# Summing attention weights and both halves of the values' product inside PSUM

## The chip, the cores and the metric

The kernel runs on one core of a Trainium2 chip. The metric is device time in microseconds (us) of one execution. Engine names in the profile: PE is the matrix engine TensorE (PEld its weight loads), DVE is VectorE, ACT is ScalarE, POOL is GpSimd, SP issues the DMAs.

## The reference, cut to what matters

Four batches of 576 tokens, eight heads of 64 features. Rotary attention comes first, then a mixer on its result: a low-rank mix over the sequence, then two dense layers with a ReLU. Only the end of the attention is touched here:

```python
scores = scores - np.max(scores, axis=-1, keepdims=True)
attn = np.exp(scores)
attn = attn / (np.sum(attn, axis=-1, keepdims=True) + 1e-09)
return np.matmul(attn, v).astype(np.float32)
```

Inputs and outputs are float32, and the mixer's weights are float64.

## The kernel before, in words

**Tiling.** A batch has four pairs of heads (index hp). A pair has five tiles of queries: four of 128 (t = 0 to 3), for each of which both heads have a softmax tile of their own, and a last one (t = NT = 4) in which the last 64 queries of both heads share one tile of 128. So a pair has nine softmax tiles, and a batch 36. For each, PE makes the scores, DVE the maximum (nmx), ACT the exponential (p), with the row sum as a second output of the same instruction (`accum_out=sm`).

**Batch 0 is plain.** With PLAIN = HV = 4 all four pairs of batch 0 take the plain path: p is transposed by PE, and the values' product runs in float32, one PE instruction for each chunk of 128 keys (5 chunks, the last of 64 keys). In the trace each float32 product stands as two passes. The values lie in v32, a float32 view of the tile va.

**Batches 1 to 3 carry halves.** ACT rounds p to float16 (the high half), POOL subtracts (the low half), and one transposing DMA turns both into nine chunks pt. The values are also split into a high and a low half of float16 (tile va, high and low side by side). The product sums high weights times (high | low) values over chunks 0 to 4, and low weights times high values over the remaining chunks. Since the 576 keys don't fill five chunks, the fifth holds 64 keys of the high weights and 64 of the low ones; the tile vb, and the upper 64 rows of va's last chunk, hold the values shifted to suit. `twice` in load_v makes them by three DMAs.

**values, lines 841 to 918.** The output tile pv is one PSUM bank: two heads, two halves, 64 columns. For each head the chunks 0 to 4 write 128 columns (two halves of 64), the other four 64. `evac` follows: rs (sum plus 1e-9, times the values' scale) and rc (its reciprocal), which need only sm; then xs, a DVE reduction that adds the two halves out of PSUM into SBUF; then xt, xs times rc, as one DVE instruction or two ACT ones, whichever the plan expects to end first. `turn` transposes xt on PE and splits it for the mix.

**load_v, lines 689 to 746.** For each of the batches 1 to 3 two raw tiles are loaded, each all 576 rows of 256 columns: a DMA of 512 KB in runs of 1 KB and one of 64 KB. ACT sums their squares, PE and DVE make the scale of that, ACT and DVE or POOL write the halves, and `twice` copies.

**What sets the order.** Up to the end of batch 3 everything is recorded by the class Plan, which knows for each instruction what memory it touches, and is then placed by a list scheduler with its own estimates of durations (`cost`), waits (`lag`) and of the DMA queue (`place`). Six passes backward and forward choose the order; each engine then runs its instructions strictly in that order. A PSUM bank is one unit of dependence: the next tile's product can't begin before the last reader of pv is done. The groups of PE instructions of one head stay together (`group`). While batch b's attention runs, the mixer of batch b - 1 fills PE; after the last batch's attention only the mixer is left.

Line 304 is `Plan.emit`, which all planned instructions share, so the rows of the profile are told apart by their tiles.

Of the kernel before, what the change touches and what calls it, by code (L numbers as in the profile page):

```python
# [21 lines left out]
#: Attention weights are carried times this, so that their low halves stay normal in float16.  # L22
PSC = 2.0**14
# [4 lines left out]
XM = 1  # L28
# [8 lines left out]
class Plan:  # L37
    """Records the program in its natural order, then emits it in the order in which a model of
    the core would start it: what comes first goes first, what comes later fills the gaps.
    Instructions depend on each other by the memory that they touch."""  # L40
# [28 lines left out]
    @contextmanager  # L69
    def later(self, level):  # L70
        """What others go before."""
        was, self.level = self.level, level
        yield
        self.level = was

    @contextmanager
    def sooner(self, steps):
        """What goes before the given number of instructions in front of it."""
        was, self.ahead = self.ahead, steps
        yield  # L80
        self.ahead = was

    def region(self, ap):
# [40 lines left out]
    def cost(calls):  # L124
        """How long they hold the engine."""
# [33 lines left out]
    def shares(calls):  # L159
        """Whether they hold the SBUF port that VectorE and GpSimd share."""  # L160
# [8 lines left out]
    def gap(self, dev, t, d):  # L169
        """The first time from t on at which dev is free for d."""  # L170
# [21 lines left out]
    def place(self, ways, before):  # L192
        """The way that is done first: when it starts, the calls, what they hold."""
        found = []
        for calls in ways:
# [5 lines left out]
            if eng == "sync":  # L201
# [7 lines left out]
                # Transfers go in the order of issue: an early issue would be in others' way.  # L209
# [25 lines left out]
    def lag(a, b):  # L235
        """From the end of an instruction to the start of one that waits for it."""
# [23 lines left out]
    def forward(self, order):  # L260
        """As early as they can be, in the given order."""
# [11 lines left out]
    def backward(self):  # L273
        """How late they could start, the last ones first."""
# [53 lines left out]
def tile_rope_attention_then_mixer(ctx, tc, qk, v, tab, u_in, v_in, w1, w2, out):  # L328
# [17 lines left out]
    def tmp(tag, shape, bufs, name):  # L346
        """A small tile for a while."""
# [29 lines left out]
    # Hidden units by chunks; before there are any, the first batch's attention has the room.  # L377
# [10 lines left out]
    # Queries of the even and the odd head, their high and low parts, the former before a pad of  # L388
    # zeros, the latter after one; keys' high parts, twice, and their low parts over zeros.
# [34 lines left out]
    def copy(o, i, engines):  # L424
        """A rounding copy."""
# [26 lines left out]
    def scaled_low(o, i, sc, hi, engines):  # L452
        """What the high half leaves of the scaled values; may overwrite these."""
# [21 lines left out]
    # Scales that are of use after the first batch's attention.  # L475
# [11 lines left out]
        # The exponent halved is the root's.  # L487
# [90 lines left out]
    def pieces(t):  # L578
        """Memory for halves of groups as they come in."""
# [6 lines left out]
    # A slot may not serve once float32 values are there.  # L586
# [7 lines left out]
    def weight(g):  # L594
        """A group from float64 to float32, and its sums of squares."""
# [55 lines left out]
    def weight_scale(w):  # L651
        """The scale of w1, or of the columns 128 (w - 1) .. of w2."""
# [36 lines left out]
    def load_v(b):  # L689
        """v in float16 halves, its rows twice over: chunk j holds the keys 128 j .. modulo S."""  # L690
        raws = []
        cuts = ((P, slice(0, NT)), (REM, slice(NT, NC)))
        first = 0
        if b == 0:
            first = HV * P
            for e in range(2):
                cc = slice(e * HV * 64, (e + 1) * HV * 64)
                r = v32[:, :, e, 0:HV * 64]
# [4 lines left out]
        hw = min(DM // 2, DM - first)  # L703
        for o in range(first, DM, max(hw, 1)):
            cc = slice(o, o + hw)
            r = next(raw_ring)[:, 0:NC * hw].rearrange("p (c d) -> p c d", d=hw)
            nc.sync.dma_start(r[:, 0:NT, :], v[b, 0:MAIN, cc].rearrange("(c p) d -> p c d", p=P))
            nc.sync.dma_start(r[0:REM, NT, :], v[b, MAIN:S, cc])
            nc.gpsimd.memset(r[REM:P, NT, :], 0.0)
            raws.append((r, cc))  # L710
        if not raws:
            return
        am = tmp("amv", [2], 2, f"amv{b}")

        def squares():
            junk = vb.rearrange("p j d -> p (j d)")[:, 0:NC * hw]
            for i, (r, cc) in enumerate(raws):
                nc.scalar.activation(
                    out=junk.rearrange("p (c d) -> p c d", d=hw), in_=r, func=AF.Square,
                    accum_out=am[:, i:i + 1],  # L720
                )
            am1 = am[:, 0:1]
            if len(raws) > 1:
                am1 = tmp("amv1", [1], 2, f"amv1{b}")
                nc.vector.tensor_reduce(out=am1, in_=am, axis=AX.X, op=ALU.add)
# [3 lines left out]
        def split(i):  # L729
            r, cc = raws[i]  # L730
            sc = state[b]["vsc"]
            for n, c in cuts:
                scaled(va[:n, c, 0, cc], r[:n, c, :], sc[:n], "AD")
            for n, c in cuts:
                scaled_low(va[:n, c, 1, cc], r[:n, c, :], sc[:n], va[:n, c, 0, cc], "DP")
# [6 lines left out]
        cols = slice(first, DM)  # L742
        squares()
        for i in range(len(raws)):
# [3 lines left out]
    def load_qk(b, hp):  # L748
        """Queries and keys of two heads."""
# [7 lines left out]
    def rope(b, hp, x):  # L757
        """Their rotation; the first batch's products are in plain float32."""
# [9 lines left out]
    def halves(b, hp, x):  # L768
        """Halves of 12 bits: contraction rows [high; low] of the queries against [high; high] and
        [low; 0] of the keys."""  # L770
        r = state[b, hp]["raw"][x]
        for e in range(2):
# [6 lines left out]
            if QS and b == 0 and x == 0:  # L779
                # The scores' scale, so that their maxima serve as they are.  # L780
# [60 lines left out]
    def values(b, hp, t, pts, sm):  # L841
        """The heads' values for one tile of queries: t, or NT for both heads' last REM."""
        plain = plain_pv(b, hp)
        nj = NC if plain else NJ
        cols = slice(hp * P, (hp + 1) * P)
        for e, pt in enumerate(pts):
            d = cols if t == NT else slice(hp * P + e * 64, hp * P + e * 64 + 64)
            o = pv.rearrange("p e k d -> p k e d") if t == NT else pv[:, e]
            with nc.group():
                for j in range(nj):  # L850
                    k = P if not plain or j < NT else REM
# [458 lines left out]
```

## Time and profile before

| | us |
|---|---|
| runs before (3), median | 709.77 |
| lowest and highest of them | 707.08, 715.2 |
| span of the profiled execution | 707.0 |
| PE busy | 661.2 (94%) |
| DVE busy | 517.0 (73%) |
| ACT busy | 399.7 (57%) |
| POOL busy | 214.1 (30%) |

The page gives no whole time for the profiled execution beside its span of 707.0; the run of 707.08 lies nearest to it, so some 0.1 us lie around the span. Busy PE is modelled: instructions overlap, so what one costs is read from the starts of its neighbours and not from its duration.

### The profile page before, as it was taken

Reading aid. Unit: us, or ns where it says so; the run is one execution under the profiler, and the core shown is the slowest. Engines: PE = TensorE matmul, PEld = TensorE weight load, DVE = VectorE, ACT = ScalarE, POOL = GpSimd, SP = SyncE. Lnnn points to the kernel's source line nnn. Section 1 sums busy time; section 2 is a strip of 40 time slices with the busy share of each in tenths; the row PEclk is TensorE's granted clock in tenths of the full one; section 3 lists DMA queues with packets and bytes.
Section 4 is the critical chain, followed back from the end, with each engine's and each line's share of the span. In section 5 each row is a group of like instructions: output and inputs, shape, how many; then the busy total and the mean of one; then the engine's idle time right before and its main releaser. Section 6 shows DMA issues by size and latency. Waiting matters only on the chain.

```text
span 707.0 us, 14026 instructions
## 1 busy us (share of the span) xinstructions
PE 661.2 (94%) x5312; PEld 538.6 (76%) x5312; DVE 517.0 (73%) x1120; ACT 399.7 (57%) x959; POOL 214.1 (30%) x201
## 2 busy tenths in 40 slices
PE   2999899997998898999999999999999999999998
PEld 1888788775776676888778878777878778777776
DVE  6888888887899998886778896777799873530220
ACT  3777677766775865645746666437766673230210
POOL 0320201012334345625434646124553452000000
PEclk9999999999899999999999999999999999999999
DMA  8767263248365558735777576427855664000000
GB/s 257 240 227 222 75 211 96 96 134 193 83 123 110 144 86 166 147 98 134 119 173 159 117 154 124 129 79 144 182 118 118 114 100 79 18 1 26 10 10 25
DMA packets 160468, 85.57 MB, mean 121 GB/s; under 512 B 131024, under 2 KB 149456, under 8 KB 160400
## 3 DMA queue, kind: packets, MB, share of 16 engines
q1 hardware_dynamic: 160400, 84.68, 50.6%
q8 instruction: 41, 0.67, 0.4%
q14 instruction: 27, 0.22, 0.1%
HBM read 41.70 MB, written 4.72 MB: 66 GB/s over the span
## 4 chain that ended last, share of the span: by engine, by line
PE 60%; DVE 20%; DMA 8%; ACT 6%; issue 4%; POOL 1%; SPq 0%; ACTq 0%; POOLq 0%; DVEq 0%
PE mm L304 40%; PE s L304 10%; PE pv L304 9%; DMA pt<-p 5%; DVE wt L304 5%; DVE raw L304 3%; ACT p L304 3%; DVE nmx L304 3%; DMA raw<-qk 1%; DVE st L304 1%; DMA x<-w 1%; DVE rs L304 1%; DVE xt L304 1%; DVE kl L304 1%; ACT room L304 1%
## 5 line engine op out<-in xcount | busy, mean ns | idle before, releaser
L304 PEld LDWEIGHTS <-wt 128*128 128x128 f16 x2688 | 253.5, 98 | 67.9 <-issue 3.0
L304 PE MATMUL mm<-room,wt 128*128 128x288 f16 (+1 forms) x1472 | 218.8, 298 | 0.1
L304 POOL TENSOR_TENSOR p<-p,p 128x576 f16<-128x576 f32 x108 | 149.1, 1385 | 195.7 <-ACT p L304 156.8
L304 PE MATMUL mm<-u,wt 128*128 128x288 f16 x1344 | 184.1, 286 | 1.9 <-DVE room L304 1.8
L304 DVE TENSOR_REDUCE nmx<-s 128x1 f32<-128x576 f32 x144 | 108.0, 752 | 28.6 <-PE s L304 25.6
L304 PE MATMUL s<-kh,st 128*128 128x288 f32 x320 | 106.8, 352 | 20.9 <-DVE st L304 14.0
L304 ACT ACTIVATE room<-mm 128x288 f16<-128x288 f32 (+3 forms) x156 | 63.0, 410 | 108.5 <-PE mm L304 107.7
L304 ACT ACTIVATE p<-s,nb 128x576 f32<-128x576 f32 x108 | 79.5, 737 | 36.7 <-DVE nb L304 33.4
L304 PE MATMUL s<-kl,st 128*128 128x288 f32 x320 | 95.4, 316 | 0.8 <-DVE kl L304 0.8
L304 DVE SCALAR_TENSOR_TENSOR room<-mm,room 128x288 f16<-128x288 f32 x112 | 50.7, 453 | 54.2 <-ACT room L304 53.4
L304 PE MATMUL pv<-va,pt 128*128 128x128 f16 (+5 forms) x760 | 83.3, 244 | 6.5 <-DMA pt<-p 6.0
L304 PEld LDWEIGHTS s<-kh,st 128*128 128x128 f32 x320 | 62.3, 197 | 32.6 <-DVE st L304 15.1
L304 ACT ACTIVATE p<-p 128x576 f16<-128x576 f32 x108 | 72.9, 681 | 11.4 <-DMA pt<-p 9.7
L304 PEld LDWEIGHTS <-pt 128*128 128x128 f16 x972 | 55.1, 98 | 18.1 <-DMA pt<-p 9.8
L304 PEld LDWEIGHTS s<-kl,st 128*128 128x128 f32 x320 | 63.0, 199 | 2.5 <-DVE kl L304 1.1
L304 DVE TENSOR_TENSOR raw<-raw,cs 128x1152 f32<-128x1152 f32 (+1 forms) x29 | 39.5, 1365 | 6.9 <-DMA raw<-qk 6.9
L304 DVE TENSOR_REDUCE xs<-pv 128x128 f32<-128x256 f32 x60 | 25.1, 419 | 24.7 <-PE pv L304 24.1
L304 DVE SCALAR_TENSOR_TENSOR ob<-mm,so,x 128x288 f32<-128x288 f32 x28 | 14.3, 510 | 37.1 <-PE mm L304 37.1
L304 PE MATMUL mm<-x,wt 128*128 128x288 f32 x128 | 35.7, 422 | 0.6 <-DVE x L304 0.6
L304 PE MATMUL pv<-vb,pt 128*128 128x64 f16 (+1 forms) x432 | 31.5, 196 | 1.7 <-DMA vb<-va 1.7
L304 PE MATMUL mm<-ident,p 128*128 128x128 f32 (+1 forms) x180 | 32.2, 294 | 0.9 <-ACT pt L304 0.5
L304 ACT ACTIVATE p<-s,nmx 128x576 f32<-128x576 f32 x36 | 26.5, 736 | 11.5 <-DVE nmx L304 11.2
(122 smaller groups left out, 816.0 us busy)
## 6 DMA issues: line engine op xcount, KB each, us to landing
raw<-qk SPq DMA_DIRECT2D x30, 576.0 KB, 4.7
wt<-w SPq DMA_DIRECT2D x23, 512.0 KB, 5.4
x<-w SPq DMA_DIRECT2D x9, 512.0 KB, 3.5
out_t<-ob SPq DMA_DIRECT2D x32, 144.0 KB, 1.8
kh<-kh SPq DMA_DIRECT2D x30, 144.0 KB, 2.6
raw<-vt SPq DMA_DIRECT2D x6, 512.0 KB, 4.9
pt<-p SPq DMA_TRANSPOSE x108, 3.3
vb<-va SPq DMA_DIRECT2D x6, 256.0 KB, 3.5
```

What stands on the lines that cost most here:

```text
L304: getattr(getattr(nc, eng), op)(*a, **k)
```

## The change

pv becomes two heads of 66 columns (64 sums, the sum of weights, a pad). va is split into two tiles: vh, whose heads are 66 columns wide with ones behind the 64 values, and vl with the low halves; vb gets the width of vh. In batches 1 to 3 each of the chunks 0 to 4 now takes two PE instructions that add into the same columns, one of 65 columns (high values and the ones) and one of 64 (low values); the other four take 65 columns. So a head's group has 14 instructions where it had nine. The exponential has no second output there, xs is gone, rs reads the sums from pv, and xt reads pv. The last tile of a plain pair takes two float32 products of 64 columns for each chunk where it took one of 128. load_v loads raw tiles of 256 rows and all columns (the last 64 rows in two parts of columns), and `twice` has four DMAs.

```diff
-    pv = psum.tile([P, 2, 2, 64], F32, name="pv")
+    pv = psum.tile([P, 2, 66], F32, name="pv")
...
-    va = cst.tile([P, NC, 2, DM], F16, name="va")
-    vb = cst.tile([P, NJ - NC, DM], F16, name="vb")
-    v32 = va.bitcast(F32)
+    vh = cst.tile([P, NC, NH, HW], F16, name="vh")
+    vl = cst.tile([P, NC, DM], F16, name="vl")
+    vb = cst.tile([P, NJ - NC, NH, HW], F16, name="vb")
...
+        for i in range(2):
+            r = next(raw_ring)[:, 0:5 * w // 2]
+            nc.sync.dma_start(
+                r[:, 0:2 * w].rearrange("p (c d) -> p c d", c=2),
+                v[b, 2 * i * P:2 * (i + 1) * P, h0 * 64:DM].rearrange("(c p) d -> p c d", p=P),
+            )
+            nc.sync.dma_start(
+                r[0:REM, 2 * w:], v[b, MAIN:S, h0 * 64 + i * w // 2:h0 * 64 + (i + 1) * w // 2]
+            )
...
         def twice():
-            nc.sync.dma_start(va[REM:P, NT, :, cols], va[0:P - REM, 0, :, cols])
-            nc.sync.dma_start(vb[REM:P, :, cols], va[0:P - REM, 1:NC, 0, cols])
-            nc.sync.dma_start(vb[0:REM, :, cols], va[P - REM:P, 0:NT, 0, cols])
+            hh, cols = slice(h0, NH), slice(h0 * 64, DM)
+            nc.sync.dma_start(vh[REM:P, NT, hh, :], vh[0:P - REM, 0, hh, :])
+            nc.sync.dma_start(vl[REM:P, NT, cols], vl[0:P - REM, 0, cols])
+            nc.sync.dma_start(vb[REM:P, :, hh, :], vh[0:P - REM, 1:NC, hh, :])
+            nc.sync.dma_start(vb[0:REM, :, hh, :], vh[P - REM:P, 0:NT, hh, :])
+        if b == (1 if HV else 0):
+            fill(vh[:, :, :, 64:HW], 1.0)
...
+            more = dict(accum_out=sm) if plain_pv(b, hp) else {}
             nc.scalar.activation(
                 out=p.rearrange("p (a b) -> p a b", a=2), in_=s[:, :, 0:HS], func=AF.Exp, bias=nb,
-                scale=1.0 if QS and b == 0 else 0.125, accum_out=sm,
+                scale=1.0 if QS and b == 0 else 0.125, **more,
             )
...
+            o = pv if t == NT else pv[:, e:e + 1]
+            mm = []
+            if plain:
+                for j in range(NC):
+                    k = P if j < NT else REM
+                    for f in range(2) if t == NT else [e]:
+                        mm.append((o[:, f if t == NT else 0, 0:64], pt[:k, j, :],
+                                   v32[f][:k, j, hp * 64:(hp + 1) * 64]))
+            else:
+                for j in range(NJ):
+                    l = pt[:, j, :]
+                    r = vh[:, j, hh, 0:65] if j < NC else vb[:, j - NC, hh, 0:65]
+                    mm.append((o[:, :, 0:65], l, r))
+                    if j < NC:
+                        r = vl[:, j, hh.start * 64:hh.stop * 64]
+                        mm.append((o[:, :, 0:64], l, r.rearrange("p (h d) -> p h d", d=64)))
...
                 nc.vector.tensor_scalar(
-                    out=rs, in0=sm, scalar1=1e-9 * PSC, scalar2=state[b]["vsc"], op0=ALU.add,
-                    op1=ALU.mult,
+                    out=rs, in0=pv[:, :, 64], scalar1=1e-9 * PSC, scalar2=state[b]["vsc"],
+                    op0=ALU.add, op1=ALU.mult,
                 )
...
-            if not plain:
-                xs = tmp("xs", [2, 64], 2, "")
-                nc.vector.tensor_reduce(
-                    out=xs, in_=pv.rearrange("p e k d -> p e d k"), axis=AX.X, op=ALU.add
-                )
-            if XM and t < NT:
-                i3 = pv[:, :, 0, :] if plain else xs
+            if t < NT:
+                i3 = pv[:, :, 0:64]
```

## Rows read from the trace of the kernel before

**Rows 1.** The page: busy time of each engine
```profile
PE 661.2 (94%) x5312; PEld 538.6 (76%) x5312; DVE 517.0 (73%) x1120; ACT 399.7 (57%) x959; POOL 214.1 (30%) x201
```
**Rows 2.** Busy time of each engine by stretches of the span
```profile
core 0: us, PE busy (x) PEld busy (x) DVE busy (x) ACT busy (x) POOL busy (x), PEclk, DMA share, GB/s
20.00:132.00 112.00, 106.90 (x720) 94.85 (x720) 96.90 (x184) 84.17 (x248) 19.27 (x23) 0.95 0.52 170
132.00:175.00 43.00, 38.53 (x181) 28.73 (x180) 34.78 (x72) 28.68 (x72) 7.84 (x6) 1.00 0.56 151
175.00:300.00 125.00, 113.98 (x886) 89.69 (x885) 112.14 (x237) 84.57 (x177) 55.12 (x49) 0.97 0.60 123
300.00:450.00 150.00, 146.31 (x1344) 119.49 (x1342) 117.73 (x280) 89.40 (x207) 70.81 (x63) 1.00 0.63 133
```
**Rows 3.** The chain's shares by tile: 20 to 132, 183 to 300, 300 to 600 us
```profile
by line: PE pv L304 29.1%; PE s L304 18.8%; PE mm L304 13.2%; DVE wt L304 5.7%; ACT p L304 5.1%; DVE nmx L304 4.5%; DVE raw L304 4.4%; DMA raw<-qk 4.3%; DVE rs L304 3.3%; issue 2.9%; ACT room L304 1.4%; DVE kl L304 1.3%; ACT pt L304 1.2%; A
...
by line: PE mm L304 24.1%; DVE wt L304 12.8%; DVE raw L304 8.2%; PE s L304 7.8%; DVE nmx L304 5.9%; PE pv L304 4.9%; DMA pt<-p 4.1%; DVE st L304 3.8%; DVE kl L304 3.7%; issue 3.2%; ACT p L304 2.7%; DVE xt L304 2.2%; DVE xs L304 2.1%; DVE ro
...
by line: PE mm L304 44.5%; PE s L304 12.3%; DMA pt<-p 8.0%; PE pv L304 7.8%; issue 4.9%; ACT p L304 4.2%; DVE nmx L304 2.3%; DVE raw L304 2.2%; DVE xt L304 1.4%; POOL p L304 1.3%; DMA kh<-kh 1.3%; DVE xs L304 0.9%; ACT room L304 0.9%; POOL 
```
**Rows 4.** The page: weight loads of the float16 products
```profile
L304 PEld LDWEIGHTS <-pt 128*128 128x128 f16 x972 | 55.1, 98 | 18.1 <-DMA pt<-p 9.8
```
**Rows 5.** Timeline of PE near 300 us: start, us to the last end, what
```profile
300.88 0.44 PE L304 MATMUL pv<-va,pt 128*128 128x128 f16 x5
301.15 0.28 PE L304 MATMUL pv<-vb,pt 128*128 128x64 f16 x4
301.27 1.14 PE L304 MATMUL mm<-room,wt 128*128 128x288 f16 x8
```
**Rows 6.** Timeline of PE near 70 us: plain products of two tiles
```profile
66.66 2.76 PE L304 MATMUL pv<-va,pt 128*128 128x64 f32 x20
...
70.94 1.47 PE L304 MATMUL pv<-va,pt 128*128 128x128 f32 x10
```
**Rows 7.** Groups of DVE by form: busy us, mean ns, idle before
```profile
L304 DVE TENSOR_REDUCE xs<-pv 128x128 f32<-128x256 f32 x60 | 25.1, 419 | 24.7 <-PE pv L304 24.1
L304 DVE TENSOR_SCALAR rs<-sm,sc_v 128x2 f32<-128x2 f32 x60 | 19.6, 328 | 2.2 <-ACT p L304 2.0
L304 DVE TENSOR_TENSOR xt<-xs,rc 128x128 f32<-128x128 f32 x34 | 16.6, 487 | 1.4
L304 DVE TENSOR_SCALAR xt<-xs,rc 64x64 f32<-64x64 f32 x12 | 3.0, 253 | 0.7
L304 DVE TENSOR_SCALAR room<-pv,rc 64x64 f32<-64x64 f32 x1 | 0.3, 268 | 0.0
```
**Rows 8.** Groups of ACT by form
```profile
L304 ACT ACTIVATE p<-s,nb 128x576 f32<-128x576 f32 x108 | 79.5, 737 | 36.7 <-DVE nb L304 33.4 <-PE pv L304 1.1 <-PE mm L304 0.6
L304 ACT ACTIVATE p<-p 128x576 f16<-128x576 f32 x108 | 72.9, 681 | 11.4 <-DMA pt<-p 9.7
L304 ACT ACTIVATION_READ_ACCUMULATOR p<-s,nb 128x1 f32 x108 | 21.1, 195 | 0.0
```
**Rows 9.** Waits of PE, 132 to 600 us: total, times, longest
```profile
PE pv L304 <- DMA vb<-va: 1.7, 1, 1.7
...
PE pv L304 <- DVE xs L304: 0.2, 1, 0.2
```
**Rows 10.** Timeline of DVE at the first evacuation of batch 1
```profile
174.70 0.42 DVE L304 TENSOR_REDUCE xs<-pv 128x128 f32<-128x256 f32 x1 [3.80 <-PE pv L304]
175.04 0.15 DVE L304 RECIPROCAL rc<-rs 128x2 f32<-128x2 f32 x1
175.16 1.22 DVE L304 TENSOR_TENSOR xt<-xs,rc 128x128 f32<-128x128 f32 x1
```
**Rows 11.** Timeline of SP: the copies of batch 1's values
```profile
166.18 0.49 SPq L304 DMA_DIRECT2D va<-va  x1
166.72 1.31 SPq L304 DMA_DIRECT2D vb<-va  x2
```

More of the change, by code (lines that the diff above doesn't have):

```diff
@@ L27 @@
 GB = 0
-XM = 1
 QS = 1
@@ L402, in tile_rope_attention_then_mixer @@
     xfs = [carve(2 * P, F32).rearrange("p (c d) -> p c d", c=2) for t in range(NC)]
-    va = cst.tile([P, NC, 2, DM], F16, name="va")
-    vb = cst.tile([P, NJ - NC, DM], F16, name="vb")
-    v32 = va.bitcast(F32)
+    NH = DM // 64
+    HW = 66
+    vh = cst.tile([P, NC, NH, HW], F16, name="vh")
+    vl = cst.tile([P, NC, DM], F16, name="vl")
+    vb = cst.tile([P, NJ - NC, NH, HW], F16, name="vb")
+    v32 = [
+        t.rearrange("p c h w -> p c (h w)")[:, :, 0:NH * 64].bitcast(F32) if e == 0 else
+        t.bitcast(F32) for e, t in enumerate((vh, vl))
+    ]
     p_all = [cst.tile([P, S], F32, name=f"p{i}") for i in range(3)]
@@ L689, in load_v @@
     def load_v(b):
[L691 to L695, printed above, removed]
+        h0 = 0
+        if b == 0 and HV:
+            h0 = 2 * HV
             for e in range(2):
                 cc = slice(e * HV * 64, (e + 1) * HV * 64)
-                r = v32[:, :, e, 0:HV * 64]
+                r = v32[e][:, :, 0:HV * 64]
                 nc.sync.dma_start(
@@ L702, in load_v @@
                 nc.sync.dma_start(r[0:REM, NT, :], v[b, MAIN:S, cc])
[L703 to L711, printed above, removed]
-            return
+        if h0 == NH:
+            return
+        hn = NH - h0
+        w = hn * 64
+        raws = []
+        for i in range(2):
[7 more added lines that the diff above has]
+            )
+            nc.gpsimd.memset(r[REM:P, 2 * w:], 0.0)
+            raws.append(r)
         am = tmp("amv", [2], 2, f"amv{b}")
         def squares():
-            junk = vb.rearrange("p j d -> p (j d)")[:, 0:NC * hw]
-            for i, (r, cc) in enumerate(raws):
+            for i, r in enumerate(raws):
                 nc.scalar.activation(
-                    out=junk.rearrange("p (c d) -> p c d", d=hw), in_=r, func=AF.Square,
-                    accum_out=am[:, i:i + 1],
-                )
[L722 to L725, printed above, removed]
+                    out=vb.rearrange("p j h w -> p (j h w)")[:, 0:5 * w // 2], in_=r,
+                    func=AF.Square, accum_out=am[:, i:i + 1],
+                )
+            am1 = tmp("amv1", [1], 2, f"amv1{b}")
+            nc.vector.tensor_reduce(out=am1, in_=am, axis=AX.X, op=ALU.add)
             sc, _ = pow2_scale(am1, f"v{b}", 15)
@@ L729, in split @@
         def split(i):
-            r, cc = raws[i]
             sc = state[b]["vsc"]
[L732 to L735, printed above, removed]
-        def twice():
-            nc.sync.dma_start(va[REM:P, NT, :, cols], va[0:P - REM, 0, :, cols])
-            nc.sync.dma_start(vb[REM:P, :, cols], va[0:P - REM, 1:NC, 0, cols])
-            nc.sync.dma_start(vb[0:REM, :, cols], va[P - REM:P, 0:NT, 0, cols])
@@ L742, in load_v @@
-        cols = slice(first, DM)
+            parts = []
+            hs = slice(h0 + i * hn // 2, h0 + (i + 1) * hn // 2)
+            r = raws[i]
+            if h0 == 0:
+                parts.append((
+                    P, vh[:, 2 * i:2 * i + 2].rearrange("p c h w -> p (c h) w")[:, :, 0:64],
+                    vl[:, 2 * i:2 * i + 2].rearrange("p c (h d) -> p (c h) d", d=64),
+                    r[:, 0:2 * w].rearrange("p (n d) -> p n d", d=64),
+                ))
+            else:
+                for c in range(2):
+                    parts.append((
+                        P, vh[:, 2 * i + c, h0:, 0:64],
+                        vl[:, 2 * i + c, h0 * 64:].rearrange("p (h d) -> p h d", d=64),
+                        r[:, c * w:(c + 1) * w].rearrange("p (n d) -> p n d", d=64),
+                    ))
@@ new lines, in split @@
+            parts.append((
+                REM, vh[0:REM, NT, hs, 0:64],
+                vl[0:REM, NT, hs.start * 64:hs.stop * 64].rearrange("p (h d) -> p h d", d=64),
+                r[0:REM, 2 * w:].rearrange("p (n d) -> p n d", d=64),
+            ))
+            for n, hi, _, x in parts:
+                scaled(hi, x, sc[:n], "AD")
+            for n, hi, lo, x in parts:
+                scaled_low(lo, x, sc[:n], hi, "DP")
+        def twice():
+            hh, cols = slice(h0, NH), slice(h0 * 64, DM)
[3 more added lines that the diff above has]
+            nc.sync.dma_start(vb[0:REM, :, hh, :], vh[P - REM:P, 0:NT, hh, :])
@@ L743, in load_v @@
+        if b == (1 if HV else 0):
+            fill(vh[:, :, :, 64:HW], 1.0)
         squares()
-        for i in range(len(raws)):
+        for i in range(2):
             split(i)
@@ L843, in values @@
         plain = plain_pv(b, hp)
-        nj = NC if plain else NJ
-        cols = slice(hp * P, (hp + 1) * P)
         for e, pt in enumerate(pts):
-            d = cols if t == NT else slice(hp * P + e * 64, hp * P + e * 64 + 64)
-            o = pv.rearrange("p e k d -> p k e d") if t == NT else pv[:, e]
-            with nc.group():
-                for j in range(nj):
-                    k = P if not plain or j < NT else REM
-                    l = pt[:k, j, :]
-                    if plain:
-                        r = v32[:k, j, slice(0, 2) if t == NT else e, hp * 64:(hp + 1) * 64]
-                        o2 = o[:, 0]
-                    else:
-                        r = va[:, j, :, d] if j < NC else vb[:, j - NC, d]
-                        o2 = o if j < NC else o[:, 0]
-                    nc.tensor.matmul(o2, l, r, start=(j == 0), stop=(j == nj - 1))
+            hh = slice(2 * hp, 2 * hp + 2) if t == NT else slice(2 * hp + e, 2 * hp + e + 1)
+            o = pv if t == NT else pv[:, e:e + 1]
[6 more added lines that the diff above has]
+                                   v32[f][:k, j, hp * 64:(hp + 1) * 64]))
+            else:
+                for j in range(NJ):
[5 more added lines that the diff above has]
+                        mm.append((o[:, :, 0:64], l, r.rearrange("p (h d) -> p h d", d=64)))
+            with nc.group():
+                for i, (o2, l, r) in enumerate(mm):
+                    nc.tensor.matmul(o2, l, r, start=(i == 0), stop=(i == len(mm) - 1))
         def evac():
@@ L892, in evac @@
             for e in range(2):
-                own = slice(0, P) if t < NT else slice(e * REM, (e + 1) * REM)
-                k = e if t < NT else 0
-                i = pv[own, e, 0, :] if plain else xs[own, e, :]
-                scaled(xt[0:n, e * 64:(e + 1) * 64], i, rc[own, k:k + 1], "DA")
+                own = slice(e * REM, (e + 1) * REM)
+                k = 0 if plain else e
+                scaled(xt[0:n, e * 64:(e + 1) * 64], pv[own, e, 0:64], rc[own, k:k + 1], "DA")
         def turn():
@@ L1004, in tiles @@
                 sm = tmp("sm", [2], 5, "")
-                if t == NT:
+                if t == NT and plain_pv(b, hp):
                     fill(sm[:, 1:2], 1.0)
```

## The prediction

> **What bounds the kernel now.** I read the busy times first: PE 661.2 of 707.0 us [rows 1]. Such a mean hides the stages, so the table by stretches came next [rows 2]. It shows three regimes. From 20 to 132 us (batch 0's plain attention) PE has work for 106.9 of 112 us, and DVE for 96.9. From 132 to 300 us (batch 1's attention beside the first batch's mixer and the conversion of the mixer's weights) PE idles 4.5 + 11.0 = 15.5 us, while DVE is busy for 112.1 of 125 us in the later part, 90%. From 300 us on PE is busy for 146.3 of 150 us, and the 150 us after those look alike. Last I read which tiles the chain runs through in each stage [rows 3]: PE's own work for 29.1 + 18.8 + 13.2 = 61% of the first; DVE's for 12.8 + 8.2 + 5.9 + 3.8 + 3.7 + 2.2 + 2.1 = 39% (what the line shows of it) of 183 to 300 us; and in 300 to 600 us almost only PE and the transposing DMAs (pt, 8.0%), with DVE at 2.3 + 2.2 + 1.4 + 0.9 = 7%. So less DVE work is worth something in batch 1, little later; more PE work costs most in batch 0 and after 300 us.
>
> **Float16 product: more instructions, the same columns.** A head's group goes from 5 x 128 + 4 x 64 = 896 columns in nine instructions to 5 x 129 + 4 x 65 = 905 columns in 14. The timeline [rows 5] gives the spacing: five of 128 columns from 300.88 to 301.15 (54 ns each), four of 64 from 301.15 to 301.27 (30 ns each), the next group at once behind them. So two of 64 cost 60 where one of 128 costs 54, and a column of ones under half a nanosecond. Before: 0.39 us. After: 14 x 30 ns and nine columns more, 0.42 us. With 3 x 4 x 8 = 96 such groups and 12 last tiles of twice the columns, which gain as little, that is 108 x 0.03 = +3 us, on PE, where nothing hides it after 300 us. The lower end is 0 (it falls into idle time of PE). The upper end is that 30 ns holds only for a short run of four; that is a rival below.
>
> **Plain last tile, batch 0.** This side effect is no part of the headline. The pair's last tile makes two float32 products of 64 columns for each chunk where it made one of 128. Ten passes of 128 columns last 1.47 us, twenty of 64 columns 2.76 us [rows 6]: a float32 pass of half the columns isn't cheaper. So each of four pairs pays 2.76 - 1.47 = 1.29 us, together 5.2 us of PE. At the share of the chain that PE has there, 61% [rows 3], I take +3.2, from 0 (all beside DVE work) to +5.2.
>
> **DVE: xs goes, its inputs move to PSUM.** 60 reductions of 419 ns, 25.1 us, go [rows 7]. rs and xt now read PSUM. The nearest rows for that price are the same multiplication from SBUF and from PSUM, 253 and 268 ns: +15 ns for each of two instructions, so 0.39 us less for each tile of queries, 7.8 us for each batch. In batch 1 the worth lies between the chain's share, 0.39 x 7.8 = 3.0, and all of it if DVE is the bound; I take the middle, -5.4. In the two later batches 15.6 x 7% = -1.1.
>
> [...]
>
> **The order inside the evacuation.** rs and rc stood ready before; now rs waits for the product, and rc and xt follow it. But xs waited there already, for 24.1 us in 21 places [rows 7], so the wait on DVE's queue changes its name and not its place; behind it stand the plan's next maximum or weight conversion, as now. At the first evacuation xs starts at 174.70 and xt at 175.16 [rows 10]; rs (328 ns mean) and rc (150) in its place take about the same 0.46. The bank is held longer: until xt ends, some 0.33 + 0.15 + 0.49 = 0.97 us in place of 0.42. What hides it is that PE has other work between the products of two tiles: it waited for xs 0.2 us in all [rows 9]. I take 0; if that cover were gone it would be 60 x 0.55 = 33 us.
>
> **ACT.** 108 reads of the accumulator, 195 ns each, 21.1 us, go from between the exponential and the rounding copy [rows 8]. They make 195 / (737 + 195 + 681) = 12% of a tile's ACT work, and the chain has ACT's p for 2.7% of 117 us and 4.2% of 300 us [rows 3], 15.8 us: -1.9. Bounds 0 and, were all on the path, -21. The nearest of the two is 0, since ACT is busy for 84.6 of 125 us there [rows 2].
>
> **load_v.** Same bytes and number of loads, same elements to split. `twice` issues four DMAs in place of three; on SP the two kinds took 0.49 and 0.65 us [rows 11], and the transposes that the products wait for queue behind them. PE waited 1.7 us for this copy once, in batch 1 [rows 9]: +0.6 there, nothing in batches 2 and 3, where the copy is early. The ones are filled once, and some fills of sm go: under 0.2 us.
>
> **Sum.** +3 + 3.2 - 5.4 - 1.1 - 1.9 + 0.6 = -1.6 us on a span of 707.0 (707.1 with what lies around it). The profiled execution is 2.7 us under the median of the runs, 709.8; put on that, 708.2. With xs gone, what is late next is the transposing DMA and the maxima (nmx). The scheduler deals a new order throughout; single waits in it, such as those of 1 to 4 us in [rows 9, 10], move either way, so I give this case 701 to 715.
>
> **Rivals.**
> 1. DVE is the bound of the whole of batch 1's stage. For it: 90% busy, 39% of the chain. [...]
> 2. Slower: PE is the bound where the passes are added. Place: the four last tiles of batch 0 and the groups after 300 us. Price: 5.2 + 3 + 0.6 = +8.8. It decides if what DVE and ACT lose only widens their idle time; below 8.8 us of relief the kernel is slower, and with none it takes 718.6 us. For it: PE at 95% and 97%. Against it: the 15.5 us in which PE idles in batch 1.
> 3. Weight loads bind in long runs. Each instruction brings a load of its own, 98 ns long [rows 4]. Four in a row at 30 ns show it hidden, 14 in a row nothing here shows. If spacing fell back to that of 128 columns, 54 ns, a group took 0.76 in place of 0.42: 108 x 0.34 = 37 us, 745 us. [...]
> 4. The longer hold of the one bank is met by PE: up to +33, near 725 if half of it is met. Against it: the 0.2 us above.
> That the change doesn't do what it says has no room: batch 0 keeps its accumulator, but in batches 1 to 3 the rows above go with the code that makes them.
>
> **How the numbers follow.** Chances: forecast 0.45, rival 1 0.28, rival 2 0.16, rival 3 0.05, rival 4 0.06. About 1%, 7.1 us, is what a measurement of this kernel can tell from no change. Faster by more (below 702.7): nearly all of rival 1 and 0.06 of the forecast, 0.33. Slower by more (above 716.9): rivals 3 and 4 and 0.10 of rival 2, 0.21. The rest, 0.46. The range 692 to 720 takes in the forecast's own, most of rival 1 and of rival 2, and leaves out about 0.16.
>
> **What would show it.** Right: groups of 14 float16 products in 0.42 us; 40 more float32 passes of 64 columns, each last tile near 2.76 us; no xs row; rs and xt from PSUM within 30 ns of before; no accumulator reads for nb tiles; DVE near 494 us, ACT near 379; PE's idle time from 132 to 300 us down from 15.5 to about 9. Wrong: a spacing over 35 ns (rival 3), waits of PE for xt or rc in its product (rival 4), 20 to 132 us longer by the whole 5 us with an unchanged stage behind it (rival 2), or idle PE in that stage below 4 us and no half clock (rival 1).

## The result, and the profile after

| | before | changed |
|---|---|---|
| median of the runs, us | 710.72 (4 runs) | 699.95 (4 runs) |
| lowest, highest | 707.08, 715.2 | 698.65, 701.23 |
| ratio to before, 95% interval | | 0.9846 (0.9804 to 0.9889) |
| span of the profiled execution | 707.0 | 698.6 |

The change makes the kernel 1.5% faster, 10.8 us between the medians. The forecast was a change too small to tell (708.2 us); the time lies inside the range (692 to 720), which covered the rivals too, but just outside the forecast's own 701 to 715, in the direction of the first rival; to an outcome faster by more than 1% the prediction had given 0.33. Two executions that took over 1.5% longer than the fastest of their kernel (718.41 us of before_xt_act, 716.78 of the kernel before) are left out of the medians and ratios below.

The page of the changed kernel, busy time of each engine, answers to [rows 1]:

```profile
PE 661.6 (95%) x5892; PEld 544.5 (78%) x5892; DVE 471.3 (67%) x1018; ACT 400.8 (57%) x901; POOL 217.5 (31%) x209
```

PE has 580 instructions more and only 0.3 us more of (modelled) busy time. DVE lost 45.7 us, twice the 23.3 that the prediction removed. ACT lost 21 us of accumulator reads and is busy as long as before: something moved onto it. The stretches of the changed kernel, with the columns of [rows 2], say where the time went:

```profile
20.00:132.00 112.00, 107.02 (x755) 95.98 (x753) 99.66 (x189) 84.12 (x249) 12.12 (x20) 0.96 0.56 181
132.00:175.00 43.00, 41.81 (x197) 31.90 (x197) 32.40 (x63) 27.36 (x65) 7.57 (x6) 0.94 0.48 131
175.00:300.00 125.00, 119.85 (x1141) 96.58 (x1140) 102.12 (x220) 90.27 (x174) 58.92 (x53) 1.00 0.62 127
300.00:450.00 150.00, 143.78 (x1486) 117.48 (x1485) 104.79 (x241) 89.35 (x185) 73.43 (x65) 1.00 0.65 139
```

From 132 to 300 us PE idled 15.5 us before and idles 1.2 + 5.1 = 6.3 now; DVE fell from 112.1 to 102.1 us in the later part. Batch 0's stage looks as before. To put times on the stages, read where the last product of a batch starts: the rows of tile pv give the first and the last start. For the plain products of batch 0 (stretch 0 to 140 us) and for batch 1 (stretch 160 to 320 us), the changed kernel:

```profile
L303 PE MATMUL pv<-vl,pt x130: 217/275/421, 23.7 to 131.8; 128*128 128x64 f32 x104, 64*128 64x64 f32 x26
...
L303 PE MATMUL pv<-vb,pt x144: 191/193/223, 172.4 to 293.9; 128*128 128x65 f16 x128, 128*128 128x130 f16 x16
```

and the kernel before:

```profile
L304 PE MATMUL pv<-va,pt x220: 218/275/473, 18.4 to 129.9; 128*128 128x64 f32 x76, 64*128 64x64 f32 x19, 128*128 128x128 f32 x12, 64*128 64x128 f32 x3
...
L304 PE MATMUL pv<-vb,pt x144: 192/193/219, 172.2 to 304.1; 128*128 128x64 f16 x128, 128*128 128x128 f16 x16
```

So batch 0 ends 1.9 us later (131.8 against 129.9), batch 1's stage shrinks from 304.1 - 129.9 = 174.2 to 293.9 - 131.8 = 162.1 us, 12.1 less, and what follows it up to the start of PE's last instruction (703.3 and 695.1) grows by 2.0. All of the gain is made in batch 1's stage.

The groups of DVE and then of ACT by form in the changed kernel, against [rows 7] and [rows 8]:

```profile
L303 DVE TENSOR_SCALAR rs<-pv,sc_v 128x2 f32<-128x2 f32 x60 | 13.0, 216 | 27.6 <-PE pv L303 26.4 <-ACT p L303 0.4
L303 DVE TENSOR_TENSOR xt<-pv,rc 128x128 f32<-128x128 f32 x7 | 2.0, 285 | 0.2
...
L303 ACT ACTIVATE xt<-pv,rc 128x64 f32<-128x64 f32 x82 | 21.3, 311 | 53.5 <-DVE rc L303 40.3 <-DVE nb L303 6.5 <-PE mm L303 2.6
```

xs is gone, and the wait for the product stands in front of rs (26.4 us, 24.1 before in front of xs). What the prediction did not see: the scheduler, offered xt on DVE or on ACT for each tile, now takes ACT nearly always. xt on DVE fell from 34 instructions of 487 ns (and 12 of 253) to seven of 285. The scheduler's own table puts an ACT instruction that reads PSUM below one that reads SBUF (line 149 of the kernel before); in the traces xt on ACT (128x64) has a mean of 311 ns from PSUM here and of 337 ns from SBUF in the kernel before. And rs lost a third of its mean. Summed over batch 1's stage, xs, rs and xt took 8.3 + 6.9 + 7.0 = 22.2 us of DVE before, and rs and xt take 4.2 + 1.4 = 5.6 now: 16.6 us less. The chain of the changed kernel, 183 to 300 and then 300 to 600 us, against [rows 3]:

```profile
by line: PE mm L303 24.7%; DMA pt<-p 11.7%; PE s L303 9.9%; PE pv L303 7.3%; ACT p L303 6.8%; issue 6.4%; DVE raw L303 6.4%; ACT wt L303 4.4%; DVE wt L303 4.4%; DVE nmx L303 3.1%; POOL p L303 2.2%; ACT xt L303 2.2%; POOL xh L303 1.3%; DVE x
...
by line: PE mm L303 42.2%; PE s L303 12.3%; DMA pt<-p 11.9%; PE pv L303 8.1%; issue 7.8%; POOL p L303 2.3%; ACT p L303 2.0%; DMA raw<-qk 1.9%; POOL raw L303 1.3%; DVE nmx L303 1.2%; DVE room L303 1.0%; SPq L303 1.0%; ACT room L303 0.9%; DVE
```

Of DVE the first line shows 6.4 + 4.4 + 3.1 = 14%, where it was 39%; xs and xt on DVE are off it, DVE's part of the weight conversion (wt) went from 12.8% to 4.4%, and the transposing DMA rose from 4.1% to 11.7%.

### The profile page after: what moved, and what is told of

Same layout as the page of the kernel before. It is cut to its first block, busy times and chain, and to the rows that moved or that the text cites. A ratio compares the mean times of both kernels' runs of the same rounds, so it can differ in the third digit from the quotient of the medians.

```text
span 698.6 us, 15048 instructions
## 1 busy us (share of the span) xinstructions
PE 661.6 (95%) x5892; PEld 544.5 (78%) x5892; DVE 471.3 (67%) x1018; ACT 400.8 (57%) x901; POOL 217.5 (31%) x209
## 4 chain that ended last, share of the span: by engine, by line
PE 60%; DVE 13%; DMA 12%; ACT 7%; issue 5%; POOL 3%; SPq 1%; ACTq 0%; POOLq 0%; DVEq 0%
PE mm L303 39%; PE s L303 11%; PE pv L303 11%; DMA pt<-p 8%; DVE wt L303 3%; ACT p L303 3%; DVE raw L303 3%; DMA raw<-qk 2%; DVE nmx L303 2%; DMA x<-w 2%; POOL p L303 2%; ACT room L303 1%; DVE kl L303 1%; ACT wt L303 1%; DVE st L303 1%
## 5 line engine op out<-in xcount | busy, mean ns | idle before, releaser
L303 PE MATMUL mm<-room,wt 128*128 128x288 f16 (+1 forms) x1472 | 216.4, 297 | 0.0
L303 POOL TENSOR_TENSOR p<-p,p 128x576 f16<-128x576 f32 x108 | 145.8, 1355 | 184.0 <-ACT p L303 139.9
L303 PE MATMUL mm<-u,wt 128*128 128x288 f16 x1344 | 181.8, 286 | 0.8 <-DVE room L303 0.6
L303 PE MATMUL s<-kh,st 128*128 128x288 f32 x320 | 105.0, 345 | 21.1 <-DVE st L303 14.4
L303 PE MATMUL pv<-vh,pt 128*128 128x65 f16 (+3 forms) x660 | 69.3, 213 | 5.6 <-DMA pt<-p 5.2
L303 PE MATMUL pv<-vl,pt 128*128 128x64 f16 (+3 forms) x670 | 70.9, 214 | 0.0
L303 PEld LDWEIGHTS <-pt 128*128 128x128 f16 x1512 | 57.9, 98 | 15.7 <-DMA pt<-p 10.3
L303 ACT ACTIVATE xt<-pv,rc 128x64 f32<-128x64 f32 (+1 forms) x103 | 27.8, 311 | 61.7 <-DVE rc L303 47.3
L303 PE MATMUL pv<-vb,pt 128*128 128x65 f16 (+1 forms) x432 | 32.0, 196 | 0.0
```

The costliest lines, as they stand in the source:

```text
L303: getattr(getattr(nc, eng), op)(*a, **k)
```

## The experiments

The theories: D, DVE's relief in batch 1's stage is the gain; A, the accumulator reads are; L, the new loads are; R, nothing but the scheduler's new order is, by chance. After the first four runs D was sharpened to S: batch 0's stage scatters by several us with any new order, and what follows it depends on DVE's work. All times are medians, and each ratio is to the kernel before on the same chip (its medians there 710.6 to 711.6).

The table below was put together after all runs. The marks are read as above, in the one profiled execution of each kernel; median and granted clock are of its runs (the clock is TensorE's mean in a run as a share of full speed; for the kernel before, of its runs beside the experiments). "Batch 1's stage" as a mark of its own was chosen then; the recorded expectations used the sum of this stage and the rest (last plain product to last PE instruction).

| kernel | median | last plain product | batch 1's stage | rest | granted clock |
|---|---|---|---|---|---|
| before | 710.7 | 129.9 | 174.2 | 399.2 | 0.986 |
| before_deal1 | 705.9 | 126.7 | 175.0 | 398.0 | 0.988 |
| before_deal2 | 711.2 | 130.7 | 176.4 | 398.8 | 0.983 |
| before_rows | 714.5 | 133.5 | 171.7 | 402.9 | 0.986 |
| before_xt_act | 707.0 | 129.1 | 167.3 | 404.5 | 0.988 |
| xs_back | 718.1 | 135.1 | 171.3 | 405.0 | 0.983 |
| after_xt_dve | 703.9 | 127.8 | 171.1 | 399.3 | 0.991 |
| changed | 700.0 | 131.8 | 162.1 | 401.2 | 0.989 |
| after_deal1 | 702.9 | 131.3 | 164.6 | 403.3 | 0.993 |
| after_deal2 | 695.0 | 132.4 | 163.2 | 397.3 | 0.999 |
| after_deal3 | 700.4 | 130.3 | 163.0 | 401.0 | 0.995 |
| acc_sums | 701.8 | 128.4 | 164.6 | 401.5 | 0.995 |
| plain_wide | 709.8 | 135.9 | 167.0 | 401.6 | 0.986 |
| wide_deal1 | 702.1 | 128.4 | 169.5 | 403.8 | 0.989 |

### xs put back

```diff
-                        mm.append((o[:, :, 0:64], l, r.rearrange("p (h d) -> p h d", d=64)))
+                        mm.append((o[:, :, 1, 0:64], l, r.rearrange("p (h d) -> p h d", d=64)))
...
+                nc.vector.tensor_reduce(
+                    out=xs, in_=pv[:, :, :, 0:64].rearrange("p e k d -> p e d k"), axis=AX.X,
+                    op=ALU.add,
+                )
```

> The changed kernel with one thing put back: high and low halves go to separate columns of the PSUM bank and the DVE reduction xs (60 x 419 ns) adds them, as before; the ones column, the 14 PE instructions of a group, the loads and the missing accumulator stay. Theory D (DVE's relief in batch 1's stage is the gain): most of the 10.8 us come back, 706 to 712 us, and PE's idle time from 132 to 300 us rises from 6 to over 11 us. Theory A (the accumulator reads on ACT are the gain): 699 to 702 us. Theory R (the scheduler's new order is the gain, by chance): no relation, anywhere from 698 to 712 us.

718.05 us, ratio 1.0089 (1.0046 to 1.0133). That is outside every expectation, D's 706 to 712 included: all of the gain goes, and 7 us more. Groups of DVE and of ACT, then the stretch of batch 1, in this kernel:

```profile
L303 DVE TENSOR_REDUCE xs<-pv 128x128 f32<-128x256 f32 x60 | 24.4, 407 | 0.0
L303 DVE TENSOR_TENSOR xt<-xs,rc 128x128 f32<-128x128 f32 x33 | 11.8, 357 | 1.9
...
L303 ACT ACTIVATE xt<-xs,rc 128x64 f32<-128x64 f32 (+1 forms) x45 | 13.9, 340 | 7.9 <-DVE xs L303 6.8 <-DVE rc L303 0.8
...
132.00:300.00 168.00, 155.08 (x1241) 122.85 (x1241) 139.15 (x296) 113.72 (x224) 63.63 (x52) 0.98 0.60 128
```

With xs back, its result lies in SBUF, and the scheduler takes xt back to DVE (33 instructions). PE's idle time in the stretch is 168.0 - 155.1 = 12.9 us against 6.3, as D said. Batch 1's stage is 9.2 us longer than in the changed kernel, batch 0 ends 3.3 us later (135.1) and the tail is 3.8 us longer; these two D doesn't explain. A is out: the accumulator reads are missing here too, and nothing is left of the gain. So is L: the new loads are here, PE waits 0.2 us for the values' copies where it had waited 1.7, and the gain is gone.

### Halves in PSUM, sums by the accumulator

```diff
-            more = dict(accum_out=sm) if plain_pv(b, hp) else {}
+            more = dict(accum_out=sm)
...
-                    r = vh[:, j, hh, 0:65] if j < NC else vb[:, j - NC, hh, 0:65]
+                    r = vh[:, j, hh, 0:64] if j < NC else vb[:, j - NC, hh, 0:64]
...
-                    out=rs, in0=pv[:, :, 64], scalar1=1e-9 * PSC, scalar2=state[b]["vsc"],
+                    out=rs, in0=sm, scalar1=1e-9 * PSC, scalar2=state[b]["vsc"],
```

> The changed kernel without the ones column: the halves still add in PSUM and xs is gone, but the sums come from the exponential's accumulator again (108 reads of 195 ns on ACT) and rs reads sm, so it can be ready before the product. Theory D: within 2 us of the changed kernel, 698 to 702 us. Theory A: 21 us of ACT work return, at least 2 to 4 us of it seen, 702 to 706 us. If rs and rc behind the product cost something in the changed kernel, this one is faster than 699 us.

701.80 us, 0.9873 (0.9831 to 0.9915), the interval overlapping that of the changed kernel. Adding the halves in PSUM has nearly the whole gain by itself. The ones column, with 21 us of ACT work saved, is worth 1.8 us by the medians, which these runs don't tell from nothing. They had a higher granted clock than the changed kernel's (0.995 against 0.989), so it may be worth more.

### The loads alone

```diff
-            r = next(raw_ring)[:, 0:NC * hw].rearrange("p (c d) -> p c d", d=hw)
-            nc.sync.dma_start(r[:, 0:NT, :], v[b, 0:MAIN, cc].rearrange("(c p) d -> p c d", p=P))
+            r = next(raw_ring)[:, 0:5 * DM // 2]
+            nc.sync.dma_start(
+                r[:, 0:2 * DM].rearrange("p (c d) -> p c d", c=2),
+                v[b, 2 * i * P:2 * (i + 1) * P, :].rearrange("(c p) d -> p c d", p=P),
+            )
```

> The kernel before with one part of the change alone: load_v loads 256 rows of all columns in runs of 2 KB (and the last 64 rows in two parts) in place of all rows of 256 columns in runs of 1 KB. Same bytes, same number of instructions. Theory D: within 2 us of the kernel before, 709 to 713 us. Theory L (the values are ready earlier, and the 1.7 us wait of PE for their copies goes): 704 to 708 us. Theory R: anywhere from 700 to 715 us.

714.51 us, 1.0044 (1.0026 to 1.0063): no gain, above D's 709 to 713 and inside R's range. PE still waited 1.1 us for the copies here, so what L supposes hardly came about in this run; it is xs_back that rules L out. It is slower by 3.5 us, and its plain products end at 133.5 in place of 129.9, though no instruction of batch 0 differs. That is the first sign of how much the order alone moves.

### Batch 0's wide product undone, in two orders

```diff
-                    for f in range(2) if t == NT else [e]:
-                        mm.append((o[:, f if t == NT else 0, 0:64], pt[:k, j, :],
-                                   v32[f][:k, j, hp * 64:(hp + 1) * 64]))
+                    f = slice(0, 2) if t == NT else slice(e, e + 1)
+                    mm.append((o[:, :, 0:64], pt[:k, j, :],
+                               v32_[:k, j, f, hp * 64:(hp + 1) * 64]))
```

> The changed kernel with the plain last tile of each pair in batch 0 undone: vh and vl lie in one tile, so that one float32 product of 128 columns serves both heads again (20 products, 40 passes fewer). The prediction's step says 5.2 us of PE go, of which 3.2 are on the path: 696 to 698 us, and the last plain product ends 3 us earlier than at 131.8 us. If the passes hide beside DVE: 699 to 701 us, with the same end. Theory R: anywhere from 695 to 710 us.

> The kernel plain_wide (the changed kernel with 128-column float32 products in the plain last tiles, 40 passes fewer) with batch 0's softmax tiles 24 instructions ahead in place of 20. The prediction's 3.2 us for these passes, if real, show as a first part shorter than the 131.3 us of the changed kernel under the same order rule: 126 to 129 us. If the passes lie beside DVE's work: 130 us or more, as far as the scatter of the order lets one tell. Second part by theory S 562 to 570 us.

709.84 us, 1.0004 (0.9967 to 1.0041), inside R's range alone, and, with 24 in place of 20 instructions ahead, 702.13 us, 0.9866 (0.9804 to 0.9928). Forty passes fewer, and the first of them is 10 us slower than the changed kernel. Its first part ends at 135.9, the second's at 128.4; the changed kernel's at 131.8 and 131.3 under the same two rules. The second fits the expectation for real passes (126 to 129), the first doesn't, and the means, 132.2 and 131.6, don't show them. Part of this scatter goes with TensorE's clock: from 20 to 132 us it was granted 0.92 in plain_wide and 0.96 in the changed kernel. It is no clean undoing either, since vh and vl share a tile here and the order behind batch 0 changed with them: wide_deal1 has 169.5 + 403.8 = 573.3 us behind batch 0, outside what S expected (562 to 570), though xs is gone. There too the clock was low: granted 0.89 from 150 to 175 us and 0.91 from 175 to 200. In that profiled execution the whole took 706.95 us, 4.8 above the kernel's median.

### Controls: the same instructions in another order

```diff
-        with plan.sooner(20 if b == 0 else 50):
+        with plan.sooner(24 if b == 0 else 50):
```

(deal1; deal2 has 20 and 56, deal3 16 and 50.)

> A control: the kernel before, with the same instructions, but the first batch's softmax tiles go before 24 instructions in front of them in the scheduler's first order in place of 20. Theory S (two parts: batch 0's stage scatters by several us with any new order, and what follows it is some 9 us shorter without xs): the last plain product ends anywhere from 126 to 137 us, and from there to the last PE instruction it takes 571 to 578 us, as in the three kernels with xs so far (573.4, 576.3, 574.6). Theory R (all is chance): that second part scatters as much as the first and falls below 570 in some.

> The same control on the changed kernel (24 in place of 20, same instructions). Theory S: the last plain product ends anywhere from 126 to 137 us, and from there to the last PE instruction it takes 562 to 570 us, as in the three kernels without xs so far (563.3, 566.1, 568.6). Theory R: that part comes out above 571.

> A control on the part behind batch 0: the kernel before with the same instructions, but the softmax tiles of batches 1 to 3 go before 56 instructions in front of them in the scheduler's first order in place of 50. Theory S (DVE's work behind batch 0 sets the second part): from the last plain product to the last PE instruction 571 to 578 us (573.0 to 574.6 so far). Theory R: outside of that, down to the changed kernel's 563 to 569.

> The same control (56 in place of 50) on the changed kernel. Theory S: second part 562 to 570 us (563.4 to 568.6 so far). Theory R: 571 us or more. The end of batch 0's products may lie anywhere from 126 to 137 us by either.

> The changed kernel with batch 0's softmax tiles 16 in place of 20 instructions ahead, same instructions. Theory S: second part 562 to 570 us, first part anywhere from 126 to 137; if the first part comes out near 127, the kernel takes 692 to 697 us and beats both. Theory R: second part 571 us or more.

The kernel before in its two new orders: 705.88 us, 0.9926 (0.99 to 0.9953), and 711.21, 1.0009 (0.9983 to 1.0035). The changed one in three: 702.93, 0.9882 (0.9807 to 0.9956); 694.99, 0.9778 (0.9721 to 0.9835); 700.36, 0.9876 (0.9803 to 0.9949). So another order, with the granted clock that came with it, moves either kernel by up to 5 us, and the groups don't meet: 705.9 to 711.2 against 695.0 to 702.9, means 709.3 and 699.6. R is out as the whole explanation. (plain_wide, at 709.8, would lie in the first group: among kernels that differ by more than the order, xs alone doesn't divide the times.) Part two was as S said but for one: 573.0 and 575.2 before; 567.9, 560.5 (1.5 below the bound) and 564.0 after. Batch 1's stage alone divides them more sharply, 174.2 to 176.4 against 162.1 to 164.6, and in the whole table the five kernels with xs and with xt largely on DVE have 171.3 to 176.4, the seven without xs and with xt largely on ACT 162.1 to 169.5. Stretch of batch 1 in before_deal2 and in after_deal2:

```profile
132.00:300.00 168.00, 152.14 (x1061) 119.77 (x1060) 144.75 (x294) 114.61 (x256) 65.34 (x59) 0.98 0.59 125
```

```profile
132.00:300.00 168.00, 158.85 (x1330) 126.18 (x1330) 140.62 (x287) 115.09 (x235) 62.36 (x53) 1.00 0.61 129
```

PE idles 15.9 us in the one and 9.2 in the other. after_deal2 is the fastest kernel of all, 2.2% under the kernel before, with one number of the scheduler changed; its interval overlaps that of the changed kernel.

What the granted clock has to do with it can be read from the runs on record. The kernel before took 707.20 us in a run with a granted clock of 0.993 and 714.77 in one with 0.983. A straight line through the 54 runs of it beside the experiments gives 0.53 us for each 0.001; what follows are estimates by that line. after_deal2 had 0.999 against the changed kernel's 0.9885, worth 5.6 us, which is all of its lead. The three kernels before had 0.983 to 0.988, the four changed ones 0.989 to 0.999: some 4 of the 9.7 us between the groups go with the clock. Whether the change raises the clock or the two only came together, no run separates. In batch 1's stage the clock matters less: from 132 to 300 us it was 0.98 in the three before and 0.99 to 1.00 in the four after, at most some 3 of the 12 us.

### xt on one engine

```diff
-                plan.add([
+                ways = [
...
-                ])
+                ]
+                plan.add(ways if plain else ways[1:])
```

(ACT alone, in the kernel before; `ways[:1]`, DVE alone, in the changed one. The last tile's two instructions follow.)

> The kernel before, with xt of batches 1 to 3 on ACT alone; xs stays on DVE. In the changed kernel the scheduler moved most of xt from DVE (46 instructions, 19.6 us, down to 7) to ACT by itself. Theory S1 (what counts is DVE work taken from batch 1's stage, whichever): from the last plain product to the end 566 to 571 us, between the two groups. Theory S2 (xs itself is what counts, xt's move is a by-effect): 572 to 578 us.

> The changed kernel, with xt of batches 1 to 3 on DVE alone, from PSUM; xs stays away. DVE gets some 40 instructions of 285 ns back, 12 us. Theory S1: from the last plain product to the end 567 to 573 us. Theory S2: 562 to 569 us.

707.04 us, 0.9957 (0.992 to 0.9994), and 703.86 us, 0.9922 (0.9879 to 0.9966). Part two: 571.7 us, a hair outside both expectations (S1 up to 571, S2 from 572), and 570.5, inside S1's 567 to 573. In batch 1's stage the runs lie in between: 167.3 us with xs on DVE and xt on ACT, 171.1 with xs gone and xt on DVE, against 174.2 and 162.1 in the two kernels that they were made from. Either relief alone shortens the stage, both together most. Each is one order only, and over all orders the groups above reach to 171.3 and 169.5, so the sizes are rough. (In the changed kernel DVE keeps ten xt, the seven of the expectation and three of the last tile.) In before_xt_act the tail got 5 us longer and gave most of it back, so what one relief is worth in the end is less certain than what it does to the stage.

## Why the prediction was right or wrong

**The frame was right.** Less DVE work was worth something in batch 1's stage and little later: the gain lies there, 12.1 us in one stage. Batch 0 grew by 1.9 (forecast +3.2) and what follows batch 1 by 2.0, where two thirds of the +3 for the products, the -1.1 and most of the -1.9 summed to some -0.6.

**The DVE term was mis-sized, and this is the step that failed.** "0.39 us less for each tile of queries, 7.8 us for each batch", taken at -5.4 in batch 1. In that stage xs, rs and xt took 16.6 us less of DVE, and over the whole kernel DVE lost 45.7 us and not 23.3. The step priced the instructions that vanish and treated the scheduler's choices as fixed. Of the 16.6 us, xs is 8.3. Another 5.6 are xt, which the scheduler moved: 46 DVE instructions of 19.6 us became ten. The last 2.7 are rs, whose mean fell from 328 to 216 ns where 15 ns more had been taken. The runs with xt held on one engine show that this choice shortens batch 1's stage by itself (174.2 to 167.3) and that its loss lengthens it (162.1 to 171.1). Why rs and xt got shorter by the mean is told in the last section.

**The weight put on DVE was about right.** The middle between the chain's share and all of it was taken, 5.4 of 7.8 us or 0.69; batch 1's stage answered 16.6 us with 12.1, or 0.73. So DVE was not the whole bound of the stage, and that the time came out on the first rival's side of the forecast (700.0 us against 708.2) is in part luck: with DVE as the whole bound 7.8 us count in full, where 16.6 went and 12.1 counted. The half clock, named in that rival's sign, did not go: the stage before had it from 174.7 to 181.5 us (granted 0.50 from 175 to 181, 0.87 over 175 to 200), and the changed kernel has it from 126.8 to 137.0 us (granted 0.50 from 127 to 137, 0.86 over 132 to 150). Of the signs named, PE's idle time of 6.3 us in 132 to 300 lies between the forecast's 9 and the rival's 4.

**Float16 products: right.** +3 us was expected for 108 groups. In the changed kernel's timeline of PE a group of 14 runs from 199.43 to 199.85, 0.42 us as forecast:

```profile
199.43 0.19 PE L303 MATMUL pv<-vh,pt 128*128 128x65 f16 x1
199.46 0.20 PE L303 MATMUL pv<-vl,pt 128*128 128x64 f16 x1
...
199.73 0.29 PE L303 MATMUL pv<-vb,pt 128*128 128x65 f16 x4
199.85 0.73 PE L303 MATMUL mm<-room,wt 128*128 128x288 f32 x2
```

The loads stay hidden in runs of 14, so the third rival is out: the spacing, 54 ns at 128 columns in [rows 5], is 30 ns at 64 and 65 here.

**Plain last tile: a smaller price than taken, and its place on the path unseen.** The group near 70 us in the changed kernel starts at 69.18 and its last pair at 71.28:

```profile
69.18 0.33 PE L303 MATMUL pv<-vh,pt 128*128 128x64 f32 x2
...
71.28 0.38 PE L303 MATMUL pv<-vl,pt 64*128 64x64 f32 x2
```

That is 71.66 - 69.18 = 2.48 us to the last end against 1.47 [rows 6], so +1.0 for each pair (2.76 had been taken in its place). On the path +3.2 were taken. The plain products end from 127.8 to 135.1 us in the seven kernels with the doubled passes and from 126.7 to 135.9 in the seven without; the scatter hides whatever it is. A good part of it goes with the clock, granted 0.92 to 1.00 in 20 to 132 us. If each microsecond at a granted 0.50 is counted as half a microsecond lost, an estimate, the means of the two sevens are 127.7 and 124.0 us instead of 131.0 and 130.6: then the passes do cost some 3 to 4 us, as forecast. The two sevens still overlap, so it isn't shown.

**Evacuation: right.** The waits of PE in 132 to 600 us, against [rows 9]:

```profile
PE pv L303 <- DMA pt<-p: 5.2, 12, 0.9
...
PE mm L303 <- ACT xt L303: 3.1, 4, 1.4
```

No product waits for the bank's reader in this stretch, so the fourth rival is out. PE waits 3.1 us for ACT's xt before a transpose; before, it waited 2.1 for ACT's and 2.0 for DVE's. The wait for the values' copies, 1.7 us, is gone, in spite of the fourth DMA that was priced at +0.6; by xs_back this is not where the gain came from.

**ACT: the size fits, unproved.** -1.9 was forecast; the kernel with the accumulator back is 1.8 us slower, within the uncertainty and at a higher granted clock. ACT as a whole is not near the 379 us named as a sign, since xt moved onto it.

**What is late next: half right.** The transposing DMA has 11.9% of the chain in 300 to 600 us, 8.0% before. The maxima (nmx) do not: they fell from 2.3% to 1.2%.

**The base.** The changed kernel's profiled execution took 700.3 us with a span of 698.6, so 1.7 us lie around a span and not the 0.1 that was taken; the kernel before's profiled execution was then some 1 us, not 2.7, under the 709.8 used, which leaves the forecast as it was, since it was put on the median. And the bound on single waits under a new order was too narrow: another order, with the clock that came with it, moves the whole by up to 5 us.

## What to carry to other kernels

Where a scheduler chooses engines by its own table, price an edit with the choices it will make anew, not with the old ones: moving an operand from SBUF to PSUM moved an instruction to another engine here, and that was a third of the DVE time saved in batch 1's stage. Read an engine's worth in the stage where its work keeps the bound engine idle, and weigh it there: of 16.6 us taken from the busiest engine 12.1 counted. And before a difference of 5 us is explained in a kernel whose order is computed, shuffle the order on both sides without changing an instruction, compare groups, and set the granted clock beside every time.

## What the runs showed of the hardware that was not expected

In these traces the small DVE instructions rs and xt have no long cases when they read PSUM; the same ones reading SBUF do. Rows of tiles rs and xt on DVE (minimum, median and maximum in ns), before and then changed:

```profile
L304 DVE TENSOR_SCALAR rs<-sm,sc_v x60: 200/220/1250, 160.3 to 590.7; 128x2 f32<-128x2 f32 x60
...
L304 DVE TENSOR_TENSOR xt<-xs,rc x34: 276/292/1431, 175.2 to 594.2; 128x128 f32<-128x128 f32 x34
```

```profile
L303 DVE TENSOR_SCALAR rs<-pv,sc_v x60: 200/219/221, 173.8 to 588.2; 128x2 f32<-128x2 f32 x60
...
L303 DVE TENSOR_TENSOR xt<-pv,rc x7: 276/283/292, 185.8 to 393.5; 128x128 f32<-128x128 f32 x7
```

The medians of these two are alike to 9 ns, so the move to PSUM costs them nothing. The small form of xt in the last tile (64x64) does cost more: a median of 252 ns from SBUF, 289 from PSUM (three instructions; 284 in the 24 of after_xt_dve), 37 ns more where 15 had been taken [rows 7]. The maxima fall from 1250 and 1431 to 221 and 292. One long case stands in [rows 10]: xt took 1.22 us from 175.16, and POOL's subtraction, in the kernel before's timeline of POOL, ran from 174.94 to 176.22:

```profile
174.94 1.28 POOL L304 TENSOR_TENSOR p<-p,p 128x576 f16<-128x576 f32 x1 [4.86 <-ACT p L304]
```

The traces of all fourteen kernels, with every rs and xt of batches 1 to 3 on DVE, settle that this is no chance. Where the input lay in SBUF and POOL had more than 0.35 us of an instruction still to run when DVE's began, all 94 were long (over 0.35 us), and at the median they ended 27 ns after POOL's did. Of the 370 that met no POOL instruction, none was long. With the input in PSUM none of 623 was long, and 206 of these began with more than 0.35 us of POOL's work ahead. acc_sums, in which rs alone goes back to reading SBUF, has the long cases of rs again (maximum 1267 ns). So these instructions waited for POOL's when all their inputs lay in SBUF, and not when one came from PSUM (xt's other input, rc, lies in SBUF either way). What in the chip makes them wait, no run here tries.
